# Attention before a two-layer MLP on one core: fewer transfers, float32 scores in the first batch, chained minima, keys copied by transfer, a cast on ScalarE

## The chip, the cores and the metric

One Trainium2 core. The metric is the device time of one execution in microseconds; the median of three runs of the kernel before is 1139.2 us (1138.72 to 1140.58).

## What is computed

Four batches, eight heads, 576 tokens, 64 columns a head; then two dense layers over the 2304 tokens with 512 columns.

```python
scores = scale * np.matmul(q, k.transpose(0, 1, 3, 2))
scores = np.where(causal, -1000000000.0, scores)
a = np.exp(scores - scores.max(-1, keepdims=True)); a /= a.sum(-1, keepdims=True) + 1e-09
local = np.matmul(a, v)
q_p = phi(q)                       # where(q > 0, q, exp(q) - 1) + 1
mem_ret = np.einsum('bhsd,bhde->bhse', q_p, M_prev)
mem_norm = np.einsum('bhsd,bhd->bhs', q_p, z_prev)[..., None] + 1e-06
attn = g * mem_ret / mem_norm + (1 - g) * local          # g = sigmoid(beta), per head
h = x @ w_in; y = np.where(h > 0, h, np.exp(np.minimum(h, 0)) - 1) @ w_out
h = y @ w2_in; out = np.maximum(0.01 * h, h) @ w2_out
```

The weights arrive as 64-bit floats and are decoded on the chip into a high and a low float32r part.

## The kernel before

**Precision by splitting.** Most products are made of float32r matmuls over a high part (a cast) and a low part (the rest), which one matmul more adds. Batch 0 (`full_v`, `ti < V32`) uses plain float32 for the weights times values, but not for the scores.

**Attention.** The work goes by pairs of heads, 16 in all. `load_qk` and `load_rest` issue a pair's loads through `load_rows` (L188): four transfers for each head of each of k, q and v, then z and M. All transfers of the kernel are issued on SP, one queue, in one order. `k_unit` (L255) transposes the keys on PE in two groups (256 and 320 rows), ScalarE casts them into both halves of `kk` (L266 and L267), VectorE makes the low part `kl` (L268). `q_unit` and `stacked` (L290) do the same for the queries, high part in one half of the 128 partitions, low part in the other (L299, L300). One score matmul over 128 partitions then gives (high + low) x high, a second one (L384) adds high x low of the keys. `score` masks and scales on VectorE with a running minimum of the negated scores (L386; the last block has two spans, whose minima L391 joins), and takes the exponential on ScalarE (L392). `norm` (L401 to L407) multiplies by the inverse sum on VectorE and GpSimd, `tr` transposes on PE, `pv` (L456) multiplies with values and memory and stores to DRAM scratch, for batches 1 to 3 in two stores of half the partitions each (L489, L490). `phi_unit` (L335) makes the memory's queries, with the gate's factor in L349 to L352.

**MLP.** The first layer's hidden columns are in 16 blocks of 128. Blocks 0 to 6 (`phase1_units`) are computed while the attention of later batches runs, once a batch is done: `u_x` loads the batch's half back from scratch, `u_h` makes a block's hidden values (`elu`, then `g_split`: high part by a cast, L582, which appears as L209, and low part on GpSimd, L583), `u_o` multiplies with the output weights after all seven. The rest of layer one and layer two follow after the attention. Decoding of the seven blocks' weights (`load_w`, L91) is spread over batch 0.

**What sets the order.** `weave` and `merge` write the units in an order of their costs, with credits for the MLP's units; a scheduler in the framework then places every engine's instructions by a simulated timeline, within priorities. So any edit can shift the order of all engines. Where a buffer is reused, it waits for its last reader: k, q and v have one buffer each.

Of the kernel before, what the change touches and what calls it, by code (L numbers as in the profile page):

```python
# [19 lines left out]
def _f(ap):  # L20
    return ap.bitcast(F32)
# [3 lines left out]
def kernel(  # L25
# [53 lines left out]
    gat = const.tile([P, H], F32, name="gat")  # L79
    omg = const.tile([P, H], F32, name="omg")  # L80
    nc.sync.dma_start(bet, beta.partition_broadcast(P))
    nc.scalar.activation(out=gat, in_=bet, func=AF.Exp, scale=-1.0)
    nc.vector.tensor_scalar(out=gat, in0=gat, scalar1=1.0, scalar2=None, op0=ALU.add)
    nc.vector.reciprocal(gat, gat)
# [52 lines left out]
    xo_scr = [dram.tile([P, NKC, tile_tok(t)[1]], F32, name=f"xo{i}") for i, t in enumerate(tiles1)]  # L137
# [31 lines left out]
    for par in range(2):  # L169
# [10 lines left out]
        nc.gpsimd.memset(d["m32"], 0.0)  # L180
        pads.append(d)
# [6 lines left out]
    def load_rows(dst, src, b, hp, ca, cb, dup):  # L188
        hs = slice(2 * hp, 2 * hp + 2)
        for j in range(2):  # L190
            h = 2 * hp + j
            cs = slice(j * D, (j + 1) * D)
            if ca == 0:
                nc.sync.dma_start(dst[:, 0:2, cs], src[b, h, 0:256, :].rearrange("(c p) d -> p c d", p=P))
            if cb == 5:
                nc.sync.dma_start(dst[0:64, 2, cs], src[b, h, 256:320, :])
                if dup:
                    nc.sync.dma_start(dst[64:128, 2, cs], src[b, h, 256:320, :])
                nc.sync.dma_start(dst[:, 3:5, cs], src[b, h, 320:576, :].rearrange("(c p) d -> p c d", p=P))
# [18 lines left out]
    class Pair:  # L218
# [12 lines left out]
        def load_qk(self):  # L231
            self.q = at.tile([P, 5, P], F32, tag="qn", bufs=1, name="qn")
            self.k = at.tile([P, 5, P], F32, tag="kn", bufs=1, name="kn")
            load_rows(self.k, k, self.b, self.hp, 0, self.cb, True)
            load_rows(self.q, q, self.b, self.hp, self.ca, self.cb, True)

        def load_rest(self):
            b, hp = self.b, self.hp
            self.v = at.tile([P, 5, P], F32, tag="vn", bufs=1, name="vn")
            load_rows(self.v, v, b, hp, 0, self.cb, True)  # L240
            self.z = at.tile([P, P], F32, tag="zb", bufs=1, name="zb")
            nc.sync.dma_start(
                self.z, z_prev[b, 2 * hp:2 * hp + 2, :].rearrange("h d -> (h d)").partition_broadcast(P)
            )
            self.mr = at.tile([P, 2, D], F32, tag="mr", bufs=1, name="mr")
            for r in range(2):
                nc.sync.dma_start(
                    self.mr[64 * r:64 * r + 64], M_prev[b, 2 * hp:2 * hp + 2].rearrange("h d e -> d h e")
                )
# [5 lines left out]
        def k_unit(self, grp):  # L255
            _, s0, n, cc = grp
            if s0 == 0:
                for j in range(2):
# [13 lines left out]
        def q_unit(self, grp):  # L272
            _, s0, n, cc = grp
            if grp is self.groups[0]:
# [60 lines left out]
        def phi_unit(self):  # L335
# [13 lines left out]
            nc.vector.tensor_scalar(out=den, in0=den, scalar1=1e-6, scalar2=None, op0=ALU.add)  # L349
            nc.vector.reciprocal(den, den)  # L350
            gb = gat[:, 2 * hp:2 * hp + 2].unsqueeze(1).to_broadcast([P, ncs, 2])
            nc.vector.tensor_tensor(out=den, in0=den, in1=gb, op=ALU.mult)  # L352
# [7 lines left out]
    class Item:  # L360
# [8 lines left out]
        def score(self, c):  # L369
# [3 lines left out]
            qs, kk, kl = pr.qs[j], pr.kk[j], pr.pad["kl", j]  # L373
# [18 lines left out]
            nc.scalar.activation(  # L392
                out=pt[0:m, 0:nk], in_=pt[0:m, 0:nk], func=AF.Exp, scale=-1.0, bias=mx[0:m, 0:1],
# [62 lines left out]
        def pv(self):  # L456
# [5 lines left out]
            pz = slice(64 - 64 * j, 128 - 64 * j)  # L462
# [26 lines left out]
            nc.sync.dma_start(xm_scr[pr.ti][ps, pr.hp, o:o + n], xp[ps])  # L489
            nc.sync.dma_start(xo_scr[pr.ti][ps, pr.hp, o:o + n], xp[pz])  # L490
# [117 lines left out]

    tail = False
# [7 lines left out]
    def phase1_units(ti):  # L617

        units = []
        for pi, (pt, o, w, _) in enumerate(parts):  # L620
# [4 lines left out]
            def u_x(pi=pi, o=o, w=w, st=st):  # L625
                xt = mtile("x", 1, F32, (NKC, NW))[:, :, 0:w]
                nc.sync.dma_start(xt, xm_scr[ti][:, :, o:o + w])
                if ti < V32:
                    st["x"] = split_x(xt, w, pi % 2)
# [3 lines left out]
                for c in range(NKC):  # L633
                    nc.sync.dma_start(x2[:, c], xo_scr[ti][:, c, o:o + w])
# [89 lines left out]
    attn.__exit__(None, None, None)  # L724
    wpb = ctx.enter_context(tc.tile_pool(name="wpb", bufs=1, side="right"))
# [149 lines left out]
```

## Time and profile before

| | us |
|---|---|
| median of 3 runs | 1139.2 |
| the profiled execution's own time | 1138.44 |
| its span, first to last instruction | 1136.4 |
| PE busy in it (share) | 1066.5 (94%) |
| DVE, ACT, POOL busy | 632.9, 517.0, 598.7 |
| mean granted clock of TensorE | 0.977 |

The span is a few us shorter than the execution's time; differences of times are taken against the latter. PE is TensorE's matmuls, PEld its weight loads, DVE VectorE, ACT ScalarE, POOL GpSimd, SPq the queue of SP from which transfers are issued. A busy PE is modelled from pipelined matmuls: starts tell more than ends. A float32 matmul leaves two records. In the chain of waits a row is what held the end at that time: an instruction, an issue, or a transfer in flight.

### The profile page before, as it was taken

The page shows a single profiled execution, that of the slowest core. Times are in us where ns is not written, and L with a number is a line of the kernel's source. Part 1 is how long each engine was busy: PE and PEld are TensorE (multiplying, and loading weights), DVE is VectorE, ACT ScalarE, POOL GpSimd, SP SyncE. Part 2 cuts the span into 40 slices and gives each one's busy share as a digit, 9 for nine tenths or more (in the row PEclk, how much of TensorE's full clock was granted, in tenths as well). Part 3 has the DMA queues.
Part 4 walks back from the last instruction along what each step waited for, and adds up shares of the span by engine and source line. Part 5 has one row for each costly group of instructions (what it writes and reads, how often), then busy time and mean ns, then how long its engine had stood idle before and what let it go on. Part 6 is the DMA issues. An engine that isn't in the chain of part 4 may idle for free.

```text
span 1136.4 us, 17760 instructions
## 1 busy us (share of the span) xinstructions
PE 1066.5 (94%) x5904; PEld 925.5 (81%) x5904; DVE 632.9 (56%) x1470; ACT 517.0 (45%) x1236; POOL 598.7 (53%) x720
## 2 busy tenths in 40 slices
PE   4887889998999999898999999999999999999998
PEld 2765779997989899886877788988888888888887
DVE  6678798779897974765656431566331232231232
ACT  5897877776787763545444232433211111111110
POOL 5778676666666752677668333575532332322222
PEclk8998889999999999998999999999999999999999
DMA  3455233444344524654364430343010020010010
GB/s 97 98 158 145 66 89 78 108 118 109 85 108 116 148 53 139 207 169 141 131 197 132 128 93 20 110 151 111 19 56 1 14 62 1 1 38 1 1 38 19
DMA packets 146906, 100.92 MB, mean 89 GB/s; under 512 B 84480, under 2 KB 140800, under 8 KB 146816
## 3 DMA queue, kind: packets, MB, share of 16 engines
q1 hardware_dynamic: 146816, 99.80, 30.7%
q8 instruction: 47, 0.77, 0.3%
q14 instruction: 43, 0.35, 0.1%
HBM read 73.80 MB, written 25.95 MB: 88 GB/s over the span
## 4 chain that ended last, share of the span: by engine, by line
PE 59%; DVE 12%; DMA 9%; POOL 7%; ACT 5%; issue 5%; SPq 3%; DVEq 0%; ACTq 0%; POOLq 0%
PE sc L823 13%; PE pm L576 13%; PE tp L576 11%; PE sc L604 5%; PE po L823 4%; PE pm L604 3%; PE po L481 3%; PE tp L413 2%; POOL w L120 2%; POOL xv L758 2%; DVE pt L386 2%; DMA wraw<-in_moe_w_out_dram 2%; PE po L604 2%; POOL gl L583 1%; DVE wm L111 1%
## 5 line engine op out<-in xcount | busy, mean ns | idle before, releaser
L583 POOL TENSOR_TENSOR gl<-e,gh 128x512 fp32r<-128x512 f32 (+2 forms) x181 | 205.1, 1136 | 334.1 <-DVE gh L209 286.8
L576 PE MATMUL tp<-xw,w 128*128 128x512 f32 (+1 forms) x504 | 146.0, 371 | 3.8 <-DVE e L590 3.8
L576 PE MATMUL pm<-xw,w 128*128 128x512 f32 (+1 forms) x496 | 142.2, 368 | 0.0
L823 PE MATMUL sc<-w,gh 128*128 128x512 f32 x448 | 136.2, 390 | 0.0
L407 POOL TENSOR_SCALAR pt<-pt,rs,omg 128x128 f32<-128x128 f32 (+4 forms) x160 | 109.4, 693 | 18.5 <-DVE rs L402 15.6
L604 PE MATMUL sc<-gh,w 128*128 128x512 f32 (+2 forms) x438 | 105.9, 343 | 6.1 <-DVE gh L209 2.5
L576 PEld LDWEIGHTS tp<-xw,w 128*128 128x128 f32 x504 | 92.7, 191 | 20.5 <-DVE e L590 4.2
L392 ACT ACTIVATE pt<-pt,mx 128x128 f32<-128x128 f32 (+4 forms) x160 | 93.0, 582 | 32.8 <-DVE mx L386 24.1
L120 POOL TENSOR_TENSOR w<-wm,w 128x512 fp32r<-128x512 f32 x64 | 84.2, 1336 | 44.6 <-ACT w L207 37.6
L576 PEld LDWEIGHTS pm<-xw,w 128*128 128x128 f32 x496 | 90.7, 188 | 16.4
L209 DVE CAST gh<-e 128x512 fp32r<-128x512 f32 (+2 forms) x181 | 92.3, 513 | 19.4 <-PE po L604 6.1
L823 PEld LDWEIGHTS sc<-w,gh 128*128 128x128 f32 x448 | 83.1, 188 | 16.5
L413 PE MATMUL tp<-ident,pt 128*128 128x128 f32 x480 | 84.6, 286 | 11.6 <-POOL pt L407 3.8
L576 PE MATMUL tp<-xv,w 128*128 128x512 f32 (+1 forms) x252 | 93.5, 371 | 0.0
L576 PE MATMUL pm<-xv,w 128*128 128x512 f32 (+1 forms) x248 | 91.4, 369 | 0.0
L386 DVE CUSTOM_DVE_ANT_0 pt<-sc,mask 128x128 f32<-128x128 f32 (+2 forms) x192 | 82.6, 446 | 15.4 <-PE sc L384 10.0
L595 ACT ACTIVATE e<-pm 128x512 f32<-128x512 f32 (+1 forms) x40 | 22.2, 556 | 147.6 <-PE pm L576 147.6
L604 PEld LDWEIGHTS sc<-gh,w 128*128 128x128 f32 x438 | 74.8, 189 | 17.1 <-DVE gh L209 3.5
L823 PE MATMUL sc<-w,gl 128*128 128x512 f32 x224 | 84.6, 389 | 0.0
L576 PE MATMUL pm<-xh,w 128*128 128x288 f32 x368 | 79.1, 305 | 5.0 <-ACT xh L207 3.2
L596 DVE TENSOR_TENSOR e<-tp,e 128x512 f32<-128x512 f32 (+1 forms) x40 | 25.5, 636 | 104.1 <-ACT e L595 104.1
L383 PE MATMUL sc<-kk,qs 128*128 128x256 f32 (+2 forms) x192 | 71.4, 377 | 12.7 <-DVE mx L386 7.4
(142 smaller groups left out, 2469.2 us busy)
## 6 DMA issues: line engine op xcount, KB each, us to landing
wraw<-in_moe_w_in_dram SPq DMA_DIRECT2D x32, 512.0 KB, 4.1
wraw<-in_moe_w_out_dram SPq DMA_DIRECT2D x32, 512.0 KB, 5.0
x<-xm SPq DMA_DIRECT2D x8, 576.0 KB, 4.6
ys<-st SPq DMA_DIRECT2D x32, 144.0 KB, 2.7
x1s<-st SPq DMA_DIRECT2D x36, 128.0 KB, 1.9
x<-x1s SPq DMA_DIRECT2D x9, 512.0 KB, 3.7
out_dram<-st SPq DMA_DIRECT2D x36, 128.0 KB, 1.7
kn<-in_k_dram SPq DMA_DIRECT2D x64, 64.0 KB, 2.2
```

Source lines behind the costliest of these rows:

```text
L120: nc.gpsimd.tensor_tensor(out=w[:, 1, a], in0=t[:, a], in1=_f(w)[:, 0, a], op=ALU.subtract)
L209: (nc.vector if eng == "V" else nc.gpsimd).tensor_copy(dst, src)
L383: nc.tensor.matmul(o, qs[:, c0:c0 + P], kk[:, k0:k0 + npad], start=True, stop=False)
L386: nc.vector.tensor_tensor_reduce(out=pt[0:m, k0:k0 + n], in0=sc[0:m, 0:n], in1=mk, op0=ALU.add, op1=ALU.min, scale=-0.125, scalar=1e38, ac ...
L392: nc.scalar.activation(out=pt[0:m, 0:nk], in_=pt[0:m, 0:nk], func=AF.Exp, scale=-1.0, bias=mx[0:m, 0:1], accum_out=self.pd["ss"][0:m, c:c ...
L407: nc.gpsimd.tensor_scalar(out=pt, in0=pt, scalar1=rs[0:m, i:i + 1], scalar2=omg[0:m, h:h + 1], op0=ALU.mult, op1=ALU.mult,)
L413: nc.tensor.transpose(dst, self.p[c][:, k0:k0 + kn], ident)
L481: nc.tensor.matmul(po[:, a:b], w, x, start=i == 0, stop=i == len(mms) - 1)
L576: nc.tensor.matmul(ph, wi[:, wj, kc, :], xx[:, kc, :], start=n_mm == 0, stop=n_mm == 11)
L583: nc.gpsimd.tensor_tensor(out=gl, in0=g, in1=_f(gh), op=ALU.subtract)
L604: nc.tensor.matmul(py, wo[:, wj, ec * P:(ec + 1) * P], gg, start=opens and f == first and n_mm == 0, stop=closes and f == last and n_mm == 2,)
L823: nc.tensor.matmul(pos[tb], gg[:, tb * P:(tb + 1) * P], wo[:, wj, :], start=f == 0 and n_mm == 0, stop=f == NF - 1 and n_mm == 2,)
```

## The change

1. `load_rows` issues two transfers per head for keys and queries (their middle 64 rows come within a block of 128, without a second copy of them), and six per pair for values; z and M are loaded for two pairs at once.
2. In batch 0 the keys are copied as float32, both heads in one tile, the queries into tiles whose other half is zero, and a span's score is one float32 matmul of just its columns. The zeros are set once on GpSimd.
3. In batches 1 to 3 the keys' second copy in the other half of `kk` is a transfer on SP in place of a ScalarE cast.
4. The second span's minimum starts from the first span's, in place of the instruction that joined them; the gate enters with the same instruction that adds 1e-6, as its inverse (`ging`).
5. `pv` of batches 1 to 3 stores all partitions in one transfer; `u_x` reads the right halves back in four transfers in place of five.
6. The MLP's cast to `gh` is on ScalarE while the attention is being written, 35 of the 56 blocks there, and stays on VectorE after it.

```diff
-    def load_rows(dst, src, b, hp, ca, cb, dup):
+    def load_rows(dst, src, b, hp, dup):
         hs = slice(2 * hp, 2 * hp + 2)
...
+        for ca, cb, r0 in ((0, 2 if dup else 3, 0), (3, 5, 320)):
+            for j in range(2):
+                nc.sync.dma_start(
+                    dst[:, ca:cb, j * D:(j + 1) * D],
+                    src[b, 2 * hp + j, r0:r0 + (cb - ca) * P, :].rearrange("(c p) d -> p c d", p=P),
+                )
+        for r in range(2 if dup else 0):
+            nc.sync.dma_start(
+                dst[64 * r:64 * r + 64, 2, :].rearrange("p (j d) -> p j d", j=2),
+                src[b, hs, 256:320, :].rearrange("j p d -> p j d"),
+            )
...
         def k_unit(self, grp):
...
+            if self.full_v:
+                nc.scalar.copy(_f(self.kk[0])[:, s0:s0 + n], tp[:, 0:n])
+                return
             for j, ps, po in self.heads():
                 kk = self.kk[j]
                 nc.scalar.copy(kk[ps, s0:s0 + n], tp[ps, 0:n])
-                nc.scalar.copy(kk[po, s0:s0 + n], tp[ps, 0:n])
+                nc.sync.dma_start(_f(kk)[po, s0:s0 + n], _f(kk)[ps, s0:s0 + n])
...
         def q_unit(self, grp):
             _, s0, n, cc = grp
+            if self.full_v:
...
+                for j, ps, po in self.heads():
+                    self.qs[j] = self.pad["q32", j]
+                    copy("V" if j else "A", self.qs[j][ps, s0:s0 + n], tp[ps, 0:n])
+                return
...
-            nc.vector.tensor_scalar(out=den, in0=den, scalar1=1e-6, scalar2=None, op0=ALU.add)
+            gb = ging[:, 2 * hp:2 * hp + 2].unsqueeze(1).to_broadcast([P, ncs, 2])
+            nc.vector.scalar_tensor_tensor(out=den, in0=den, scalar=1e-6, in1=gb, op0=ALU.add, op1=ALU.mult)
             nc.vector.reciprocal(den, den)
...
-            nc.vector.tensor_tensor(out=den, in0=den, in1=gb, op=ALU.mult)
...
-                nc.tensor.matmul(o, qs[:, c0:c0 + P], kk[:, k0:k0 + npad], start=True, stop=False)
-                nc.tensor.matmul(o, qs[:, c0:c0 + P], kl[:, k0:k0 + npad], start=False, stop=True)
+                if pr.full_v:
+                    nc.tensor.matmul(sc[:, 0:n], qs[:, c0:c0 + P], _f(kk)[:, k0:k0 + n], start=True, stop=True)
+                else:
+                    nc.tensor.matmul(o, qs[:, c0:c0 + P], kk[:, k0:k0 + npad], start=True, stop=False)
+                    nc.tensor.matmul(o, qs[:, c0:c0 + P], kl[:, k0:k0 + npad], start=False, stop=True)
...
-                    scale=-0.125, scalar=1e38, accum_out=mx[0:m, i:i + 1],
+                    scale=-0.125, scalar=mx[0:m, 0:1] if i else 1e38, accum_out=mx[0:m, i:i + 1],
...
-            if c == 4:
-                nc.vector.tensor_tensor(out=mx[:, 0:1], in0=mx[:, 0:1], in1=mx[:, 1:2], op=ALU.min)
...
-            nc.sync.dma_start(xm_scr[pr.ti][ps, pr.hp, o:o + n], xp[ps])
-            nc.sync.dma_start(xo_scr[pr.ti][ps, pr.hp, o:o + n], xp[pz])
+            nc.sync.dma_start(xq_scr[pr.ti][j][:, pr.hp, o:o + n], xp)
...
-        copy(E_GH, gh, g)
+        copy("A" if attending else E_GH, gh, g)
...
-                for c in range(NKC):
-                    nc.sync.dma_start(x2[:, c], xo_scr[ti][:, c, o:o + w])
+                for j in range(2):
+                    ps, pz = slice(64 * j, 64 * j + 64), slice(64 - 64 * j, 128 - 64 * j)
+                    nc.sync.dma_start(xt[ps], xq_scr[ti][j][ps, :, o:o + w])
+                    nc.sync.dma_start(x2[ps], xq_scr[ti][j][pz, :, o:o + w])
```

The queue of SP at its start, before (kn, qn, vn are a pair's keys, queries and values, wraw the raw weights):

```order
L194 DMA kn<-in_k_dram 128x2x64
L196 DMA kn<-in_k_dram 64x64
L198 DMA kn<-in_k_dram 64x64
L199 DMA kn<-in_k_dram 128x2x64
...
L196 DMA qn<-in_q_dram 64x64
L198 DMA qn<-in_q_dram 64x64
L199 DMA qn<-in_q_dram 128x2x64
L194 DMA vn<-in_v_dram 128x2x64
L101 DMA wraw<-in_moe_w_in_dram 128x4x256
```

and with the change:

```order
L199 DMA kn<-in_k_dram 128x3x64 x2
L199 DMA kn<-in_k_dram 128x2x64 x2
L199 DMA qn<-in_q_dram 128x3x64 x2
L199 DMA qn<-in_q_dram 128x2x64 x2
L199 DMA vn<-in_v_dram 128x2x64
L102 DMA wraw<-in_moe_w_in_dram 128x4x256
```

Ahead of the first value and weight transfers stand 8 loads in place of 16.

The same queue where the second pair of batch 1 is prepared, with the change (kk is the keys' tile, xm the scratch of batch 0):

```order
L286 DMA kk_1483<-kk_1483 64x256
L286 DMA kk_1484<-kk_1484 64x256
L199 DMA kn<-in_k_dram 128x3x64 x2
L199 DMA kn<-in_k_dram 128x2x64
L286 DMA kk_1483<-kk_1483 64x320
L514 DMA xm_80<-xp 64x320
L286 DMA kk_1484<-kk_1484 64x320
L199 DMA kn<-in_k_dram 128x2x64
```

The four copies stand between the next pair's key loads and a store of an earlier item.

ScalarE's queue at the first pair, before:

```order
L266 CAST kk_211<-sc 64x256
L267 CAST kk_211<-sc 64x256
L266 CAST kk_212<-sc 64x256
L267 CAST kk_212<-sc 64x256
L266 CAST kk_211<-sc 64x320
L267 CAST kk_211<-sc 64x320
L266 CAST kk_212<-sc 64x320
L267 CAST kk_212<-sc 64x320
L299 CAST qs_232<-sc 64x256
L299 CAST qs_233<-sc 64x256
```

and with the change:

```order
L281 COPY kk_214<-sc 128x256
L281 COPY kk_214<-sc 128x320
L226 COPY q_0_161<-sc 64x256
L370 ACTIVATE ph_e<-qn 128x640
L226 COPY q_0_161<-sc 64x320
```

Eight casts of keys became two copies, and each query group has one copy here, the other on VectorE.

## Rows read from the trace of the kernel before

**Rows 1.** Busy time by stretch: us, busy us (instructions), clock, DMA share, GB/s.

```profile
0.00:161.00 161.00, 123.64 (x612) 96.64 (x613) 120.76 (x336) 125.67 (x324) 113.55 (x173) 0.88 0.43 111
161.00:440.00 279.00, 265.02 (x1980) 254.07 (x1979) 232.43 (x700) 203.80 (x573) 180.35 (x278) 0.99 0.39 99
640.00:1136.00 496.00, 490.79 (x2356) 414.06 (x2354) 157.38 (x283) 96.70 (x179) 173.77 (x160) 1.00 0.13 42
```

**Rows 2.** Chain of waits, 0 to 161 us: start us, us, what.

```profile
1.16 0.42 SPq L194
...
10.41 0.47 SPq L194
10.92 4.51 DMA wraw<-in_moe_w_in_dram
...
28.47 0.25 SPq L194
...
60.04 7.73 DMA wraw<-in_moe_w_out_dram
...
81.31 5.04 DMA wraw<-in_moe_w_out_dram
...
125.52 0.62 SPq L198
```

**Rows 3.** Chain of waits, 161 to 440 us, shares by line.

```profile
by line: PE pm L604 14.0%; PE po L481 8.7%; PE pm L576 7.8%; PE tp L413 6.6%; issue 4.9%; DVE pt L386 4.0%; DMA x<-xm 3.4%; PE sc L383 3.0%; PE sc L384 2.8%; ACT pt L392 2.5%; DVE qs L300 2.0%; DVE al L216 2.0%; PE tp L576 1.8%; DVE dl L216
```

**Rows 4.** Timeline from 9 us: start, us, engine, line, what, [idle before <- releaser].

```profile
10.68 1.09 PE L296 MATMUL sc<-ident,qn 128*128 128x128 f32 x3 [2.53 <-DMA qn<-in_q_dram]
```

**Rows 5.** Groups by line: count, busy us, mean ns, idle before it.

```profile
L173 POOL MEMSET kl<- 64x576 f32 x4 | 2.3, 573 | 0.2
...
L267 ACT CAST kk<-sc 64x256 fp32r<-64x256 f32 (+1 forms) x64 | 25.2, 394 | 0.8
...
L268 DVE TENSOR_TENSOR kl<-sc,kk 64x256 fp32r<-64x256 f32 (+1 forms) x64 | 28.8, 451 | 12.4 <-ACT kk L267 11.6
...
L488 DVE COPY xp<-po 128x256 f32<-128x256 f32 (+1 forms) x48 | 21.5, 448 | 5.1 <-PE po L481 4.7
...
L391 DVE TENSOR_TENSOR mx<-mx 128x1 f32<-128x1 f32 x32 | 13.7, 429 | 0.1
```

**Rows 6.** Waits, 0 to 161 us: total us, times, longest us.

```profile
POOL rs L401 <- ACT pt L392: 21.2, 12, 7.8
...
ACT wm L109 <- DMA wraw<-in_moe_w_out_dram: 4.2, 3, 1.9
```

**Rows 7.** Timeline of PE from 41.5 us.

```profile
41.88 1.03 PE L481 MATMUL pm<-d,vv 128*128 128x256 f32 x4
42.74 0.49 PE L413 MATMUL tp<-ident,pt 128*128 128x128 f32 x3
...
43.31 0.28 PE L383 MATMUL sc<-kk,qs 128*128 128x256 f32 x1
43.43 0.28 PE L384 MATMUL sc<-kl,qs 128*128 128x256 f32 x1
```

**Rows 8.** Groups of DVE by line and shape, 161 to 440 us.

```profile
L209 DVE CAST gh<-e 128x288 fp32r<-128x288 f32 x41 | 17.7, 434 | 0.4
```

**Rows 9.** Transfers of the whole run: count, KB each, median us to landing.

```profile
xm<-xp SPq DMA_DIRECT2D x32, 64.0 KB, 2.0
```

**Rows 10.** Timeline, first and twelfth pair of batches 1 to 3.

```profile
112.49 0.42 ACT L267 CAST kk<-sc 64x320 fp32r<-64x320 f32 x1
...
114.14 0.47 PE L383 MATMUL sc<-kk,qs 128*128 128x256 f32 x1
...
395.41 0.42 ACT L267 CAST kk<-sc 64x320 fp32r<-64x320 f32 x1
...
400.72 0.28 PE L383 MATMUL sc<-kk,qs 128*128 128x256 f32 x1
```

**Rows 11.** Waits of SP's queue, 161 to 440 us: total us, times, longest.

```profile
SPq L489 <- DVE mx L386: 9.8, 10, 3.9
```

More of the change, by code (lines that the diff above doesn't have):

```diff
@@ L79 @@
     gat = const.tile([P, H], F32, name="gat")
+    ging = const.tile([P, H], F32, name="ging")
     omg = const.tile([P, H], F32, name="omg")
     nc.sync.dma_start(bet, beta.partition_broadcast(P))
-    nc.scalar.activation(out=gat, in_=bet, func=AF.Exp, scale=-1.0)
-    nc.vector.tensor_scalar(out=gat, in0=gat, scalar1=1.0, scalar2=None, op0=ALU.add)
-    nc.vector.reciprocal(gat, gat)
+    nc.scalar.activation(out=ging, in_=bet, func=AF.Exp, scale=-1.0)
+    nc.vector.tensor_scalar(out=ging, in0=ging, scalar1=1.0, scalar2=None, op0=ALU.add)
+    nc.vector.reciprocal(gat, ging)
     nc.vector.tensor_scalar(out=omg, in0=gat, scalar1=-1.0, scalar2=1.0, op0=ALU.mult, op1=ALU.add)
@@ L136 @@
     xm_scr = [dram.tile([P, NKC, tile_tok(t)[1]], F32, name=f"xm{i}") for i, t in enumerate(tiles1)]
-    xo_scr = [dram.tile([P, NKC, tile_tok(t)[1]], F32, name=f"xo{i}") for i, t in enumerate(tiles1)]
+    xq_scr = [
+        [dram.tile([P, NKC, tile_tok(t)[1]], F32, name=f"xq{i}_{j}") for j in range(2)] for i, t in enumerate(tiles1)
+    ]
     x_scr = [
@@ L180 @@
         nc.gpsimd.memset(d["m32"], 0.0)
+        for j in range(2):
+            d["q32", j] = pools["wst"].tile([P, S], F32, tag=f"q32{j}_{par}", name=f"q32{j}_{par}")
+            nc.gpsimd.memset(d["q32", j][64 - 64 * j:128 - 64 * j], 0.0)
         pads.append(d)
@@ L239, in load_rest @@
             self.v = at.tile([P, 5, P], F32, tag="vn", bufs=1, name="vn")
[L240 to L249, printed above, removed]
+            load_rows(self.v, v, b, hp, True)
+            if hp % 2 == 0:
+                load_memory(b, 2 * hp)
+            zb, mr = memory_in[b, hp]
+            h0 = 2 * (hp % 2)
+            self.z = zb[:, h0 * D:h0 * D + P]
+            self.mr = mr[:, h0:h0 + 2, :]
         def heads(self):
@@ L257, in k_unit @@
             if s0 == 0:
-                for j in range(2):
+                for j in range(1 if self.full_v else 2):
                     self.kk[j] = at.tile([P, S], F32R, tag=f"kk{j}", bufs=2, name=f"kk{j}")
@@ L273, in q_unit @@
             _, s0, n, cc = grp
+            if self.full_v:
+                tp = bank("sc")
+                for c in cc:
+                    c0, m = CH[c]
+                    nc.tensor.transpose(tp[:, c0 - s0:c0 - s0 + P], self.q[:, c, :], ident)
+                for j, ps, po in self.heads():
+                    self.qs[j] = self.pad["q32", j]
+                    copy("V" if j else "A", self.qs[j][ps, s0:s0 + n], tp[ps, 0:n])
+                return
             if grp is self.groups[0]:
@@ L387, in score @@
                     out=pt[0:m, k0:k0 + n], in0=sc[0:m, 0:n], in1=mk, op0=ALU.add, op1=ALU.min,
-                    scale=-0.125, scalar=1e38, accum_out=mx[0:m, i:i + 1],
+                    scale=-0.125, scalar=mx[0:m, 0:1] if i else 1e38, accum_out=mx[0:m, i:i + 1],
                 )
-            if c == 4:
-                nc.vector.tensor_tensor(out=mx[:, 0:1], in0=mx[:, 0:1], in1=mx[:, 1:2], op=ALU.min)
+            last = len(spans) - 1
             nc.scalar.activation(
-                out=pt[0:m, 0:nk], in_=pt[0:m, 0:nk], func=AF.Exp, scale=-1.0, bias=mx[0:m, 0:1],
+                out=pt[0:m, 0:nk], in_=pt[0:m, 0:nk], func=AF.Exp, scale=-1.0, bias=mx[0:m, last:last + 1],
                 accum_out=self.pd["ss"][0:m, c:c + 1],
@@ L607, in o_mm @@
                 )
+    attending = True
     tail = False
@@ L724 @@
     attn.__exit__(None, None, None)
+    attending = False
     wpb = ctx.enter_context(tc.tile_pool(name="wpb", bufs=1, side="right"))
```

29 lines of the change are left out of this document (13 added, 16 removed).

## The prediction

> **What bounds the kernel now.** I began with busy times by stretch [rows 1]. From 640 to 1136 us PE is busy 490.8 of 496 us: there the kernel is its matmuls, and no edit touches them. Between 440 and 640 us lies the rest of the MLP's first layer with its weight decode; the change touches none of that either. So what can move lies in the first 440 us, and whatever is gained there moves the rest forward unchanged, as the work of both later stretches is the same.
>
> Stretch A (0 to 161 us, until the first matmul of the MLP) has no full engine: DVE 120.8, ACT 125.7, POOL 113.6 and PE 123.6 of 161 us, at a granted clock of 0.88. An engine's share does not say here what a saving is worth; the chain of waits does [rows 2]. I summed its pieces from 0 to 161 us by engine: 31.7 us DVE (54 pieces), 24.1 us SPq (46), 33.9 us transfers in flight (9), 22.1 us PE (35), 21.0 us ACT (37), 8.6 us POOL (5). The reader is to see that SP, which computes nothing, holds the end for 24 us by issuing alone. It issues one transfer after another, 0.42 to 0.59 us each, and the weights that the decode waits for stand in the same queue: the row at 60.04 is 7.73 us in which the chain is only a weight transfer, the row at 81.31 another 5.04 us, the one at 10.92 another 4.51 us.
>
> Stretch B (161 to 440 us, batches 1 to 3 woven with the MLP) has PE busy 265.0 of 279 us, so at most some 14 us of plain idleness are to be had, more where a matmul waits behind another's operand. Its chain (the 200 longest of 780 pieces, its lines in [rows 3]) still has 40.7 us DVE, 14.9 us ACT, 19.7 us transfers and 7.0 us SPq beside 90.1 us PE.
>
> **The change, part by part, stretch A.**
>
> *Fewer transfers.* A pair's keys, queries and values take 8 issues each now and 4, 4 and 6 then; z and M take 3 each pair now and 3 each second pair then. At the start 18 pieces of SPq up to 10.9 us stand in the chain, 9.4 us or 0.52 us each, the first and the last of them in [rows 2]; the first q transpose waits 2.53 us for its transfer and starts at 10.68 [rows 4]. The order shows 8 issues instead of 16 ahead of the first value and weight transfer: 8 x 0.52 = **-4.2 us**. The four added clears on POOL cost 573 ns each like the present kl clears [rows 5], 2.3 us, beside POOL's longest wait for an exponential, 7.8 us, which is its first [rows 6]: nothing, and 2.3 us if that cover goes. After the start 21 more pieces of loads (L194 to L199) lie in the chain, 11.1 us, first and last in [rows 2]; 24 loads become 14, so 10/24 of it: **-4.6 us**. The bounds are nothing (another row of the queue takes each place) and the whole 11.1 us. The rows say that an issue holds SP for about half a microsecond, and I take that. The Trainium skill ("DMA: Bandwidth & Descriptors", Anatomy of one DMA — SWDGE (gpsimd) path) gives about 50 ns for the sequencer's dispatch, for transfers issued by GpSimd; by that the two terms would shrink from 8.8 to about 0.8 us and the forecast would be 1124. The rows of SP contradict 50 ns tenfold, and the measurement decides.
>
> The weight transfers in the chain (17.3 us in three pieces) come earlier when fewer loads stand ahead. How much of their landing then disappears behind other work no row shows: nothing at one end, 12.8 us (the two later pieces) at the other. I take **-3 us**, near the low end, since ACT waited only 4.2 us in all for them [rows 6].
>
> *Float32 scores in batch 0.* Per pair, ACT loses 8 key casts and 2 of 4 query casts, 394 ns each, and gets 2 full-width copies of the same columns, priced alike: -3.2 us. DVE loses 4 kl and 4 qs subtractions, 451 ns each, and gets 2 query copies, 448 ns as the xp copy: -2.7 us [rows 5]. *Chained minima* take away one instruction of 429 ns per head: -0.9 us a pair. *The gate's factor* takes away one small instruction on ten columns, priced like a minimum: -0.4 us. Over four pairs that is 12.6 us ACT and 16.0 us DVE. With some 2.5 pairs of batch 1 prepared in A (ACT loses 4 second key casts, DVE the minima and the gate) it is 16.5 of ACT's 125.7 us (13%) and 19 of DVE's 120.8 us (16%). Taken from their pieces of the chain in the same shares: 2.7 + 5.1 = **-7.8 us**. The bounds are 0, if other waits step in, and 35.5 us, if all of it was on the path.
>
> PE pays. Two float32 matmuls of 256 columns take 0.86 us from start to start (four records, 41.88 to 42.74), so 0.43 us each; a float32r one takes 0.12 us (43.31 to 43.43) [rows 7]. A head's six spans are 1856 columns twice now, 2 x 1856/256 x 0.12 = 1.74 us, and 1728 columns in float32 then, 1728/256 x 0.43 = 2.90 us. Eight heads: +9.3 us of PE. PE is 22.1 of A's 161 us in the chain, 14%, so I count **+1.3 us**; the bounds are 0 and 9.3 us at this clock.
>
> A: -4.2 - 4.6 - 3 - 7.8 + 1.3 = **-18.3 us**.
>
> **Stretch B.** 35 of the 56 gh casts go from DVE to ACT: 35 x 434 ns [rows 8] = 15.2 us off DVE. Minima and gate over 9.5 pairs: 9.5 x 1.29 = 12.2 us. Together 27.4 of DVE's 232.4 us, 12%, of 40.7 us in the chain: **-4.9 us**. On ACT the casts add 15.2 us and the 4 second key casts of 9.5 pairs take away 15.0 us: 0; behind it a cast can now queue behind exponentials, covered because a block's g is used only after all seven. On SP a pair has 35 transfers now (27 loads, 8 stores) and 23.5 then (15.5 loads, 4 copies of keys, 4 stores): a third less of 7.0 us, **-2.3 us**. Against it stands the keys' second copy, 394 ns on ACT today, by transfer then. No row shows a transfer inside the chip's memory; the nearest is 2.0 us for an xp store of the same 64 KB [rows 9], plus an issue of 0.5 us. Today the second-half copy is ready 3.6 us before the pair's first score in the mean of 12 pairs, 1.2 us in the first of them (112.91 to 114.14) and 4.9 us in the last (395.83 to 400.72) [rows 10], and scores over the first 256 keys need only the first half, so most of it is hidden: I take **+2 us**, between 0 and the +29 us of the rival below. B: **-5 us**.
>
> Sum: -23 us against the profiled execution's 1138.4 us (span 1136.4). That run stands 0.8 us under the median, 1139.2, and against the median it is **1116 us**.
>
> **The rivals.** *POOL paces A.* POOL loses nothing, and it is 113.6 of 161 us busy. If its normalisation is what every item waits for, the ACT and DVE savings turn into waits on it, and only the two SP terms remain: 1139.2 - 8.8 = 1130. For it: 71% busy, and next in size. Against it: it idles 21.2 us waiting for the exponentials [rows 6] and is 8.6 us of A's chain.
>
> *The keys' copy comes late (slower).* SP serves its queue in order. A copy stands behind whatever SP is waiting for: in B it stood 10 times before an xp store (L489), up to 3.9 us at once [rows 11]. A copy held 3.9 us, issued (0.5) and landed (2.0) takes 6.4 us against 0.4 us today, so it is 6.0 us later; the mean lead covers 3.6 us of that, and PE would stand 2.4 us in each of 12 pairs, with the MLP's matmuls queued behind: +29 us. With the other terms (-25) that is 1143. It decides from a mean hold of about 3.6 us, where the loss in a pair reaches 25/12 = 2.1 us. For it: nothing in the queue goes around a wait. Against it: fewer loads stand in the queue, and 3.9 us is the longest hold there, not the mean (9.8 us in 10 times).
>
> *The savings were hidden anyway.* The order of every engine moves, the pieces of the chain are replaced by their neighbours, and the time stays within the noise: 1139.
>
> **How the numbers follow.** First case 0.62 (1116), POOL 0.18 (1130), late copies 0.13 (1143), hidden 0.07 (1139). Low end: the SP, weight and ACT/DVE terms at twice their value, 1096. High end: up to the hidden case, 1140; the late copies stay out. About 0.2%, 2.3 us, is what a measurement of this kernel can tell from no change. Faster 0.80, same 0.07, slower 0.13.
>
> **What would show it.** Right: the first matmul of the MLP starts at about 143 us, SPq falls under 15 us in the chain of A, ACT and DVE lose 13 and 16% there, PE in the float32 scores takes about 2.9 us a head, the stretch after the attention keeps its length. Wrong: scores waiting for a kk transfer for over 1 us a pair, POOL over 85% busy in A, or a first MLP matmul still at 160 us.

## The result and the profile after

The changed kernel takes 1123.2 us (median of 4 runs, 1122.8 to 1124.8) beside 1139.9 us for the kernel before: a ratio of 0.9859, with a 95% interval of 0.9844 to 0.9874. That is 1.4% faster. Of its stages, by the profiled executions:

| us | before | after | difference |
|---|---|---|---|
| first matmul of the MLP (end of stretch A) | 161.1 | 132.8 | -28.3 |
| last store of the attention issued | 442.8 | 419.1 | -23.7 |
| from there to the end | 693.6 | 702.3 | +8.7 |
| span | 1136.4 | 1121.4 | -15.0 |

So the attention gave 23.7 us, and 8.7 us were lost again in a stretch whose instructions the change does not touch. Busy time by stretch after [rows 1] (us, then busy us and instructions of PE, PEld, DVE, ACT and POOL, then clock, DMA share, GB/s):

```profile
0.00:133.00 133.00, 108.87 (x551) 81.45 (x552) 94.03 (x261) 96.35 (x248) 110.14 (x163) 0.97 0.52 137
133.00:420.00 287.00, 274.76 (x2063) 266.86 (x2063) 228.72 (x669) 209.72 (x605) 187.31 (x293) 0.98 0.42 108
...
620.00:1121.00 501.00, 495.68 (x2345) 411.13 (x2343) 154.65 (x282) 95.30 (x177) 172.75 (x159) 1.00 0.13 42
```

Three things are to be seen. POOL, 113.6 of 161 us before, is now 110.1 of 133 us (83%) and the fullest engine of stretch A. PE's granted clock there is 0.97 in place of 0.88, so more of the stretch runs at 2.4 GHz and less at 1.2. And the boundary between the stretches has moved within the work: 550 records of matmuls lie before the first MLP matmul now, 612 before, as the third pair of batch 1 is only partly prepared by then. Over both stretches PE has 2614 records in either kernel. Up to 443 us it was busy 391.7 us and idle 51.3 (the window of [rows 1] ends 3 us earlier); now, up to 420 us, 383.6 and 36.4. So 15 of these 23 us are idle time gone, and 8 are PE's busy time, although the float32 scores take longer. The clock alone does not explain the 8: run e2 below, in the order of the kernel before, has 0.94 in its first 160 us, and its attention ends only 2.4 us sooner (440.4). What does was not found.

The chain of waits of stretch A after (start us, us, what) [rows 2]:

```profile
5.31 0.47 SPq L199
...
5.82 0.47 SPq L102
...
6.88 5.37 DMA wraw<-in_moe_w_out_dram
...
46.93 6.12 POOL pt L436 x5
...
64.10 4.22 POOL w L121 x2
...
126.89 5.42 DMA x<-xm
```

Summed over all its pieces by engine, before and after: SPq 24.3 and 14.0 us, transfers 33.9 and 16.6, DVE 33.7 and 6.2, ACT 21.7 and 18.8, PE 26.8 and 35.3, POOL 8.6 and 32.0. Beside PE the chain now runs through the normalisation (L436) and the weights' low parts (L121) on POOL, where it ran through VectorE, loads and weight transfers. POOL's wait for exponentials, 21.2 us before [rows 6], has nearly gone; ScalarE's for weights has shrunk a little (waits, 0 to 133 us: total us, times, longest):

```profile
POOL rs L430 <- ACT pt L421: 3.7, 2, 2.6
...
ACT wm L110 <- DMA wraw<-in_moe_w_out_dram: 2.9, 3, 1.6
```

The start went as forecast. PE's timeline from 3 us (start, us, engine, line, what, [idle before <- releaser]) [rows 4]:

```profile
4.15 1.51 PE L279 MATMUL sc<-ident,kn 128*128 128x128 f32 x5 [4.15 <-DMA kn<-in_k_dram]
6.38 1.57 PE L297 MATMUL sc<-ident,qn 128*128 128x128 f32 x5 [0.73 <-DMA qn<-in_q_dram]
7.75 2.56 PE L411 MATMUL sc<-kk,q 128*128 128x128 f32 x6
```

The first q transpose starts at 6.38 us in place of 10.68, the first score at 7.75. The keys' copies by transfer land when they were expected to (count, KB each, median us to landing) [rows 9], and never late. The tightest pair is the second of batch 1 (timeline of all engines): its last copy, of the keys behind the first 256, is issued at 118.84 and lands at 120.93, and its first score, which needs only the first 256 keys, starts at 120.34. No score waits for such a copy anywhere in the waits of the kernel.

```profile
kk<-kk SPq DMA_DIRECT2D x24, 80.0 KB, 2.1
kk<-kk SPq DMA_DIRECT2D x24, 64.0 KB, 2.0
```

```profile
118.84 0.55 SPq L286 DMA_DIRECT2D kk<-kk  x1
...
120.34 0.37 PE L413 MATMUL sc<-kk,qs 128*128 128x256 f32 x1
```

Where are the 8.7 us? In the later stretch, the same matmuls are slower one by one, at a granted clock of 1.00 in both. Groups of PE by line and shape from 520 to 680 us, of before (count, busy us, mean ns of one):

```profile
L576 PE MATMUL pm<-xw,w 128*128 128x512 f32 x112 | 35.1, 389 | 0.0
```

and of the changed kernel:

```profile
L603 PE MATMUL pm<-xw,w 128*128 128x512 f32 x113 | 35.9, 395 | 0.0
```

From start to start the difference is the same: 0.227 us before, 0.233 us now, in the mean over the 512-column matmuls of the rest of layer one. In layer two it goes by block. The median distance from start to start, in ns, of the matmuls with x of blocks 0 to 15, second group of tokens, worked out from the starts in the traces:

```
before 227 227 227 227 227 227 227 227 227 227 227 227 227 227 227 227
after  230 227 227 227 227 227 227 234 234 234 234 234 234 234 234 234
```

Blocks 7 to 15 are slow, and all of layer one's rest has those blocks too. The kernel takes its tiles from two ends of the on-chip memory, `side="left"` and `side="right"`. The weights of these blocks lie on the right; x, gh and the first seven blocks' weights lie on the left. The one part of the change that moves them is the 32-byte tile `ging`: it pushed all that lies on the left 32 bytes further.

### The profile page after: what moved, and what is told of

Its sections match the earlier page's. It is cut to its first block, busy times and chain, and to the rows that moved or that the text cites. A ratio compares the mean times of both kernels' runs of the same rounds, so it can differ in the third digit from the quotient of the medians.

```text
span 1121.4 us, 17423 instructions
## 1 busy us (share of the span) xinstructions
PE 1066.8 (95%) x5904; PEld 917.1 (82%) x5904; DVE 600.0 (54%) x1363; ACT 493.9 (44%) x1191; POOL 599.9 (53%) x724
## 4 chain that ended last, share of the span: by engine, by line
PE 69%; DMA 9%; POOL 7%; DVE 6%; ACT 4%; issue 4%; SPq 2%; DVEq 0%; POOLq 0%; ACTq 0%
PE pm L603 16%; PE sc L854 14%; PE tp L603 12%; PE sc L631 5%; PE po L854 4%; PE pm L631 4%; PE po L509 3%; PE tp L442 3%; POOL w L121 2%; DMA x<-xq 2%; PE po L631 2%; PE pm L509 2%; DMA wraw<-in_moe_w_out_dram 1%; PE sc L413 1%; PE sc L414 1%
## 5 line engine op out<-in xcount | busy, mean ns | idle before, releaser
L610 POOL TENSOR_TENSOR gl<-e,gh 128x512 fp32r<-128x512 f32 (+2 forms) x181 | 202.0, 1119 | 348.7 <-DVE gh L228 304.3
L603 PE MATMUL tp<-xw,w 128*128 128x512 f32 (+1 forms) x504 | 147.0, 374 | 5.5 <-DVE e L617 5.5
L603 PE MATMUL pm<-xw,w 128*128 128x512 f32 (+1 forms) x496 | 143.8, 371 | 0.0
L854 PE MATMUL sc<-w,gh 128*128 128x512 f32 x448 | 137.7, 393 | 0.0
L436 POOL TENSOR_SCALAR pt<-pt,rs,omg 128x128 f32<-128x128 f32 (+4 forms) x160 | 107.2, 679 | 19.4 <-DVE rs L431 15.8
L603 PEld LDWEIGHTS tp<-xw,w 128*128 128x128 f32 x504 | 92.2, 190 | 24.3 <-DVE e L617 6.0
L121 POOL TENSOR_TENSOR w<-wm,w 128x512 fp32r<-128x512 f32 x64 | 87.5, 1387 | 37.3 <-ACT w L226 37.1
L603 PEld LDWEIGHTS pm<-xw,w 128*128 128x128 f32 x496 | 90.5, 188 | 18.4
L421 ACT ACTIVATE pt<-pt,mx 128x128 f32<-128x128 f32 (+4 forms) x160 | 93.4, 585 | 23.4 <-DVE mx L416 21.7
L603 PE MATMUL tp<-xv,w 128*128 128x512 f32 (+1 forms) x252 | 93.9, 373 | 0.0
L603 PE MATMUL pm<-xv,w 128*128 128x512 f32 (+1 forms) x248 | 92.0, 371 | 0.0
L228 DVE CAST gh<-e 128x512 fp32r<-128x512 f32 (+2 forms) x146 | 76.5, 527 | 20.4 <-PE po L631 7.5
L442 PE MATMUL tp<-ident,pt 128*128 128x128 f32 x480 | 79.3, 277 | 8.3 <-ACT ah L232 3.2
L623 DVE TENSOR_TENSOR e<-pm,e 128x512 f32<-128x512 f32 (+1 forms) x40 | 25.5, 636 | 106.7 <-ACT e L622 106.6
L603 PE MATMUL pm<-xh,w 128*128 128x288 f32 x368 | 80.1, 303 | 2.1 <-ACT xh L226 1.7
L416 DVE CUSTOM_DVE_ANT_0 pt<-sc,mask 128x128 f32<-128x128 f32 (+4 forms) x160 | 69.0, 448 | 12.1 <-PE tp L442 6.0
```

The source lines that it names most:

```text
L121: nc.gpsimd.tensor_tensor(out=w[:, 1, a], in0=t[:, a], in1=_f(w)[:, 0, a], op=ALU.subtract)
L228: (nc.vector if eng == "V" else nc.gpsimd).tensor_copy(dst, src)
L416: nc.vector.tensor_tensor_reduce(out=pt[0:m, k0:k0 + n], in0=sc[0:m, 0:n], in1=mk, op0=ALU.add, op1=ALU.min, scale=-0.125, scalar=mx[0:m, ...
L421: nc.scalar.activation(out=pt[0:m, 0:nk], in_=pt[0:m, 0:nk], func=AF.Exp, scale=-1.0, bias=mx[0:m, last:last + 1], accum_out=self.pd["ss"] ...
L436: nc.gpsimd.tensor_scalar(out=pt, in0=pt, scalar1=rs[0:m, i:i + 1], scalar2=omg[0:m, h:h + 1], op0=ALU.mult, op1=ALU.mult,)
L442: nc.tensor.transpose(dst, self.p[c][:, k0:k0 + kn], ident)
```

## The experiments

Ratios are to the kernel before, timed beside each run, and the changed kernel stands at 0.9859. Stage times are those of each run's profile.

**Is it the position? (e1, e2, e3, e5, e6.)** An unused tile moves the left side in the changed kernel (e1) and in the kernel before (e2):

```diff
-    omg = const.tile([P, H], F32, name="omg")
+    omg = const.tile([P, H], F32, name="omg"); pad = const.tile([P, H], F32, name="pad"); nc.gpsimd.memset(pad, 0.0)
```

e3 has the same tile on the right side, ahead of the attention's tiles; e6 has 96 bytes on the left (`[P, 3 * H]`); e5 needs no new tile:

```diff
-    ging = const.tile([P, H], F32, name="ging")
+    ging = bet
```

Apart from one clear on GpSimd, the order of every engine's instructions is that of the kernel it is made from (e5 has no such clear).

> The changed kernel with one more unused tile of 32 bytes per partition among the constants, on the side where the first seven blocks' weights, x and gh lie; every engine's order is the same but for one clear on GpSimd. The change's own new 32-byte tile (ging) had moved all that lies on that side from 32 to 0 mod 64 bytes, while the weights of blocks 7 to 15 on the other side stayed at 32 mod 64; in the trace of the changed kernel the matmuls that pair the two sides start about 5 to 7 ns further apart than before. Theory position (operands of one matmul at unlike places in 64 bytes go slower): both sides are at 32 mod 64 again, 512-column matmuls start 0.227 us apart everywhere, and the time falls by 8 to 13 us, to 1110 to 1115. Rival (the wider spacing comes from something else, as the activity before it or the new order of the work): 1123 within 2 us, spacing as in the changed kernel.

> The kernel before with an unused tile of 32 bytes per partition among the constants; nothing else differs but one clear on GpSimd. Theory position: the left side moves to 0 mod 64, the matmuls that pair it with blocks 7 to 15 start 0.23 to 0.235 us apart in place of 0.227, and the time rises by 8 to 13 us, to 1147 to 1153. Rival (the spacing comes from the new order): no change, 1139.5 within 2 us.

> The changed kernel with the unused 32-byte tile on the other side, ahead of the attention's tiles, the weights of blocks 7 to 15 and x: now both sides are at 0 mod 64. Theory position as a difference between the two operands: fast, 1110 to 1115, spacing 0.227 everywhere, as with the tile on the left. Rival within it, position by itself (a tile at 0 mod 64 is slow, whatever the other): no better than the changed kernel, 1123 or up to 10 us slower. Rival order: 1123 within 2 us.

> The changed kernel with the gate's inverse kept in the tile of beta, so that no new tile is there and every later tile of the left side lies where it lay in the kernel before (96 mod 128 bytes, as the weights of blocks 7 to 15 on the other side). So far the stretch from the last attention store to the end took 694 us with the two sides at the same place in 128 bytes (the kernel before), 702 and 702 us at 32 bytes apart, 698 and 699 us at 64 bytes apart. Theory position: 694 us again, 512-column matmuls 0.227 us apart everywhere, 1114 to 1118. Rival (a new order of the work is what slows that stretch in the changed kernel): 1121 to 1124.

> The changed kernel with an unused tile of 96 bytes among the constants: the left side lies 128 bytes further than in the kernel before, at the same place in 128 bytes as the other side, and not in 256. Theory period of 128 bytes: as e5, 1114 to 1118, spacing 0.227 everywhere. Rival (only the very addresses of before are fast, a longer period): 1119 to 1124, spacing wider in some of the blocks.

| run | left side against right side, bytes from before | ns of one (L603 pm<-xw) | from the last store to the end, us | time, us | ratio (95%) |
|---|---|---|---|---|---|
| before | 0 | 389 | 693.6 | 1139.9 | 1 |
| after | +32 | 395 | 702.3 | 1123.2 | 0.9859 (0.9844 to 0.9874) |
| e1 | +64 | 391 | 698.3 | 1122.4 | 0.9863 (0.9844 to 0.9882) |
| e2, from before | +32 | 395 | 701.3 | 1144.6 | 1.0062 (1.0044 to 1.0079) |
| e3 | +64 | 391 | 699.4 | 1120.6 | 0.9847 (0.9827 to 0.9866) |
| e5 | 0 | 389 | 694.0 | 1118.1 | 0.9819 (0.9800 to 0.9838) |
| e6 | +128 | 394 | 702.8 | 1124.7 | 0.9874 (0.9854 to 0.9895) |

The rows behind the third column, for e2 and for e5:

```profile
L576 PE MATMUL pm<-xw,w 128*128 128x512 f32 x112 | 35.8, 395 | 0.0
```

```profile
L603 PE MATMUL pm<-xw,w 128*128 128x512 f32 x120 | 37.4, 389 | 0.0
```

e2 settles that it is position: an unused tile of 32 bytes costs the kernel before 0.6% (7 us), with its order unchanged, and its later stretch grows from 693.6 to 701.3 us. e5 settles that it explains the loss: with the left side back in place the stretch is 694.0 us, the time falls to 1118.1 us, and the interval lies wholly below that of the changed kernel. By the ratios the whole kernel gains some 4.6 us of the 8.3 that the stretch gives back in the profiled execution; in e1, e3, e5 and e6 the last store comes 1 to 3 us later than in the changed kernel's profile, with the same order. **By its median e5 is the fastest version.** e1 and e3 have different positions, but the same difference between the two sides (a tile on the right, which is filled from its other end, counts like one on the left), the same 391 ns, and block for block the same steps in layer two: what counts is how the sides lie to each other. My rule was too simple, though. I had expected e1 to be as fast as e5 (same place in 64 bytes); it recovered half of what the stretch had lost (in layer two its blocks 7 to 15 lie between 229 and 233 ns), and nothing that its total could tell. Then I expected e6 to be fast (same place in 128 bytes); it is as slow as the changed kernel. What period the positions have, and what in the chip waits, stays open.

**The keys' copy (e4, e9) and the gh cast (e8, e7).** e4 takes the copies back to ScalarE:

```diff
                 nc.scalar.copy(kk[ps, s0:s0 + n], tp[ps, 0:n])
-                nc.sync.dma_start(_f(kk)[po, s0:s0 + n], _f(kk)[ps, s0:s0 + n])
+                nc.scalar.copy(kk[po, s0:s0 + n], tp[ps, 0:n])
```

> The changed kernel with the keys' second copy in batches 1 to 3 made by ScalarE again in place of the transfer (48 copies of about 392 ns, 18.8 us on ScalarE; 48 issues fewer on SP). Theory hidden: the trace shows no score that waits for such a transfer, so the transfer costs nothing and gives ScalarE some room: undoing it costs 0 to 5 us, 1123 to 1128. Rival late copies: the copies stand behind stores on SP and hold scores back, so undoing it gains over 3 us, under 1120.

e4: 1137.6 us (1134.0 to 1142.7), ratio 0.9993 (0.9978 to 1.0007). That is 1.3%, 15 us, slower than the changed kernel: nearly its whole gain is gone. Stretch A is nearly as before the edit (134.4 us), the loss lies in batches 1 to 3, whose last store comes at 437.2 in place of 419.1 us. Neither theory had it: the direction is that of the hidden case, the size three times its upper end. Late copies are out. e8 puts the gh cast on VectorE again, e7 both:

```diff
-        copy("A" if attending else E_GH, gh, g)
+        copy(E_GH, gh, g)
```

> The changed kernel with the gh cast on VectorE throughout; the keys' copies stay a transfer. The prediction's terms: 35 casts of 434 ns go back to VectorE, 15.2 us, of which its share of the chain gives about 3 us: 1126. Theory ScalarE's load: ScalarE gets still freer by 15 us, so no loss or a gain, 1116 to 1124. Rival VectorE's load: 1128 or more.

> The changed kernel with the keys' second copy on ScalarE and the gh cast on VectorE throughout, both as before. The run with the copies alone on ScalarE again was 1.3% slower than the changed kernel. Theory ScalarE's load (with both jobs ScalarE is too late for matmuls that wait on it): the gh casts are taken off it again, so most of that loss goes, 1122 to 1128. Rival (the loss is in the copies themselves, as they hold the score bank and kk, whatever else ScalarE does): 1133 or more.

e8: 1129.2 us, ratio 0.9916 (0.9898 to 0.9934), 6.5 us slower than the changed kernel, as the rival of VectorE's load had it. Only 1.7 us of it stand at the attention's last store and some 1.3 are ten more matmuls left over for later (0.13 us each). Most of the rest are waits of PE where layer one ends, in code that the edit does not touch: from 520 to 640 us it is idle for 2.9 us in the changed kernel and for 7.2 in e8 (PE's busy time by stretch, first of the changed kernel, then of e8):

```profile
520.00:560.00 40.00, 39.74 (x171) 1.00 0.50 158
560.00:640.00 80.00, 77.36 (x329) 1.00 0.39 125
```

```profile
520.00:560.00 40.00, 37.79 (x161) 1.00 0.46 137
560.00:640.00 80.00, 75.06 (x318) 1.00 0.40 129
```

e7: 1134.8 us, ratio 0.9959 (0.9945 to 0.9974), so taking the casts off ScalarE again does not bring back what the copies cost; the rival's 1133 holds. The four kernels form a table. With the keys' copies by transfer, the gh cast on ScalarE gains 6.5 us (0.9916 to 0.9859); with the copies on ScalarE it loses 4 us (0.9959 to 0.9993). So the cast is worth something on ScalarE only once the copies are off it. Busy time from 134.4 to 438 us in e4:

```profile
134.40:438.00 303.60, 281.90 (x2078) 272.75 (x2079) 238.04 (x677) 227.23 (x648) 187.90 (x296) 0.97 0.36 93
```

and from 133 to 431 us in e7:

```profile
133.00:431.00 298.00, 278.67 (x2063) 270.11 (x2064) 245.02 (x716) 219.13 (x614) 189.87 (x296) 0.97 0.37 95
```

ScalarE is 227.2 of 303.6 us busy in e4, 75%, and 219.1 of 298 in e7, 74%; in the changed kernel it is 73%. No engine is full, and still the copies' 18.8 us on ScalarE cost 15 us with the casts on it (e4 beside the changed kernel) and 5 without them (e7 beside e8). Together the two parts are worth 11 us (e7 beside the changed kernel). e9 asks whether it is ScalarE's load or the place of the copies, which stood ahead of the second head's cast and so kept the bank of the transposed keys:

```diff
                 nc.scalar.copy(kk[ps, s0:s0 + n], tp[ps, 0:n])
-                nc.sync.dma_start(_f(kk)[po, s0:s0 + n], _f(kk)[ps, s0:s0 + n])
...
+            for j, ps, po in self.heads():
+                kk = self.kk[j]
+                nc.scalar.copy(kk[po, s0:s0 + n], _f(kk)[ps, s0:s0 + n])
```

> The changed kernel with the keys' second copy on ScalarE again, but read from kk and behind both first casts, so that the bank of the transposed keys comes free as soon as with the transfer; ScalarE's load is that of e4 (1.3% slower than the changed kernel). Theory bank (the copies held a score bank and the low parts behind them): most of the loss goes, 1123 to 1128. Rival ScalarE (the copies stand in its queue ahead of what PE and the others wait for, wherever they read from): 1132 or more.

e9: 1130.3 us (1125.6 to 1133.5), ratio 0.9916 (0.9891 to 0.9941), between the two. With the same copies on ScalarE as in e4, the later place, and reading from `kk`, win back over half of the loss (the bank's theory), and 6.5 us stay (ScalarE's). The scheduler also moves the instructions of all engines with each of the edits e4 and e7 to e12, and no run tells a part's own worth from that of the new order. So I take this split, and the size of each single part, as rough; e8 shows some 4 us of waits in a stretch whose code is the same.

**The loads (e11).** `load_rows`, `load_qk` and `load_rest` as before, eight transfers a pair for each of k, q and v, and z and M for each pair.

```diff
...
-            load_rows(self.k, k, self.b, self.hp, False)
-            load_rows(self.q, q, self.b, self.hp, False)
+            load_rows(self.k, k, self.b, self.hp, 0, self.cb, True)
+            load_rows(self.q, q, self.b, self.hp, self.ca, self.cb, True)
...
```

> The changed kernel with the loads of k, q, v, z and M as before (27 a pair in place of 15.5 on average). The prediction's terms: 4.2 us at the start, 4.6 later in the first stretch, 3 for weights that land later, some 2 in the stretch of batches 1 to 3: 1137. Rival (after the start another row of the queue or another engine holds the chain): 1124 to 1129.

e11: 1159.0 us (1158.5 to 1159.9), ratio 1.0172 (1.0151 to 1.0192). That is 36 us slower than the changed kernel, 2.6 times my terms, and even slower than the kernel before. Stretch A ends at 166.2 us, where it ended at 161.1 before. Its busy times:

```profile
0.00:166.00 166.00, 129.36 (x623) 97.16 (x624) 108.41 (x297) 108.85 (x282) 124.89 (x181) 0.90 0.43 113
```

VectorE and ScalarE have 12 and 17 us less to do in A than before [rows 1], and A is not a microsecond shorter. That the loads alone bring A back to its old length points at the queue of SP as what held it. Counted over its issues up to 130 us, SP spends 104 us issuing in the kernel before (192 transfers), 108 in e11 (195) and 79 in the changed kernel (153). A piece of e11's chain of waits shows it, four issues to a head (two heads here), each some half a microsecond, one behind the other:

```profile
25.53 0.47 SPq L200
...
26.05 0.48 SPq L202
...
26.57 0.59 SPq L204
...
27.20 0.59 SPq L205
...
27.89 0.41 SPq L200
...
28.35 0.48 SPq L202
...
28.87 0.60 SPq L204
...
29.51 0.59 SPq L205
```

The transfers of the changed kernel are no slower to issue, though they carry more (instructions of line 199 up to 130 us: count, ns min/median/max, first and last start):

```profile
L199 SPq DMA_DIRECT2D kn<-in_k_dram x28: 368/480/1872, 1.2 to 119.4; - x28
L199 SPq DMA_DIRECT2D qn<-in_q_dram x28: 369/474/520, 3.2 to 125.0; - x28
```

Its 28 issues for keys are seven pairs' loads, at four a pair; in e11 a pair takes eight. And it goes on behind the attention: e11 has 476 matmuls of the first seven blocks left then, the changed kernel 393; at 0.13 us each that is 11 us. This is also why e11 is slower than the kernel before: the last store comes at 442.1 us, as there (442.8), but 87 more matmuls are left behind it (11 us), and the wider spacing of the blocks 7 to 15 is still in it. The same loads issued from a second queue, which would tell SP's issuing from the landing of the transfers, were not tried.

**The scores and the minima (e10, e12).** e10 makes the scores of batch 0 from float32r parts again, with the keys' second copy on ScalarE there; e12 has the separate minimum and the separate product with the gate again (of each edit the main lines):

```diff
...
-                if pr.full_v:
-                    nc.tensor.matmul(sc[:, 0:n], qs[:, c0:c0 + P], _f(kk)[:, k0:k0 + n], start=True, stop=True)
-                else:
-                    nc.tensor.matmul(o, qs[:, c0:c0 + P], kk[:, k0:k0 + npad], start=True, stop=False)
-                    nc.tensor.matmul(o, qs[:, c0:c0 + P], kl[:, k0:k0 + npad], start=False, stop=True)
+                nc.tensor.matmul(o, qs[:, c0:c0 + P], kk[:, k0:k0 + npad], start=True, stop=False)
+                nc.tensor.matmul(o, qs[:, c0:c0 + P], kl[:, k0:k0 + npad], start=False, stop=True)
```

```diff
-            gb = ging[:, 2 * hp:2 * hp + 2].unsqueeze(1).to_broadcast([P, ncs, 2])
-            nc.vector.scalar_tensor_tensor(out=den, in0=den, scalar=1e-6, in1=gb, op0=ALU.add, op1=ALU.mult)
+            nc.vector.tensor_scalar(out=den, in0=den, scalar1=1e-6, scalar2=None, op0=ALU.add)
...
+            nc.vector.tensor_tensor(out=den, in0=den, in1=gb, op=ALU.mult)
...
-                    scale=-0.125, scalar=mx[0:m, 0:1] if i else 1e38, accum_out=mx[0:m, i:i + 1],
+                    scale=-0.125, scalar=1e38, accum_out=mx[0:m, i:i + 1],
...
+            if c == 4:
+                nc.vector.tensor_tensor(out=mx[:, 0:1], in0=mx[:, 0:1], in1=mx[:, 1:2], op=ALU.min)
...
```

> The changed kernel with the scores of batch 0 by float32r parts again (casts, low parts and two matmuls a span as before, the second copy on ScalarE there). The prediction's terms: ScalarE gets 12.6 us and VectorE 10.8 us more in the first stretch, of which their shares of the chain are 2.1 and 2.9 us; PE loses 9.3 us, 1.3 us of the chain: 1127. Rival PE (the float32 scores hold the first stretch): faster than the changed kernel, under 1120. Rival full weight (ScalarE and VectorE each hold the stretch): 1133 or more.

> The changed kernel with the separate minimum of the last block's two spans and the separate product with the gate, as before: 48 small VectorE instructions of some 0.43 us more, 20.6 us. The prediction's terms: 2.3 us in the first stretch and 2.2 in that of batches 1 to 3: 1128. Rival hidden: 1121 to 1125.

e10: 1133.7 us (1128.2 to 1134.9), ratio 0.9940 (0.9916 to 0.9963), 9 us slower than the changed kernel. The first MLP matmul comes at 141.1 us, 8.3 later. So the float32 scores gain although PE pays for them, which rules out that they hold A. The size, over twice my term of 3.7 us, is at the bound that I had set for the full weight of ScalarE and VectorE; but as in e8 some of it are waits of PE where layer one ends (idle for 6.2 us from 520 to 640 us, in place of 2.9), and the second copies on ScalarE are in it too. e12: 1134.3 us (1130.6 to 1140.2), ratio 0.9953 (0.9934 to 0.9972), 10.7 us slower; A ends at 137.7 us, and the attention's last store comes 8.3 us later. Hidden is out: 20.6 us of small instructions, on an engine that is 71 and 80% busy in the changed kernel's two stretches, cost half their length.

## Why the prediction was right, and where it was not

The forecast was 1116 us (1096 to 1140) with 0.80 for faster; the result, 1123.2, lies in the range and on the side foreseen.

- **The sum held to the end of the attention and failed behind it.** I forecast -23 us there, and it is -23.7. The step that failed is "whatever is gained there moves the rest forward unchanged". e2 and e5 show why: the change added a tile, the tile moved the operands of some 2000 later matmuls against each other, and that stretch lost 8.7 us. Without that displacement (e5) the kernel takes 1118.1 us, 2 us from the forecast. That the sum up to there is met so closely is luck in good part: its two halves missed by 10 us each, in opposite directions, and some of the single parts by more, as the next points show.
- **The split into A and B was off.** A fell by 28.3 us (forecast 18.3), B grew by 4.6 (forecast -5), and the first MLP matmul came at 132.8 us, not 143. Some of A's fall is the boundary: most of a pair of batch 1 that was prepared in A is prepared in B now, 62 records of matmuls. Of the signs that I named, VectorE and ScalarE lost 22 and 23% of their time in A in place of 16 and 13, for that reason too. The price of the float32 scores held: a span of 288 columns takes 0.49 us from start to start, which is 2.9 us a head. The stretch after the attention did not keep its length.
- **Loads, -8.8 us in A, with 3 us for the weights and most of 2.3 us in B.** The start gave what was priced: 4.3 us at the first q transpose (10.68 to 6.38) for 4.2. SPq fell to 14.0 us in A's chain, under the 15 named. But as a whole the term was far too small: 14 us with its share of B, where e11 shows 36 when the loads alone are put back. I summed SP's 24 us in the chain and took a share of them; I did not count that SP issued for 104 of the first 130 us, and called the stretch one without a full engine. The Trainium skill ("DMA: Bandwidth & Descriptors", Anatomy of one DMA — SWDGE (gpsimd) path) has about 50 ns for the dispatch on GpSimd's path. By it the term would have shrunk; the issues on SP, which is another path, took 0.41 to 0.60 us in the rows above, and the term grew.
- **The keys' copy, +2 us.** The sign was wrong. Its landing time (2.0 us) was right, its lead was enough, and no score waits for it. But I set ScalarE's balance to 0, 15.2 us of casts against 15.0 us of copies, and put at nothing that the copies on ScalarE keep the bank of the transposed keys: e4 shows 15 us, of which e9 lays over half on that bank. The two belong together, as e7 and e8 show.
- **ACT and DVE, -7.8 us in A and -4.9 in B, and PE +1.3.** Taken back one at a time these parts cost 9 us (scores, 3.7 by my terms), 10.7 (minima and gate, 4.5) and 6.5 (gh, 2.7). The direction held, the sizes were two to three times too small. A share of the chain is what is visible on the path before; it supposes that the next engine in line does not gain with it, which was not tested. In B the share was also taken of the 200 longest pieces alone: they hold 40.7 us of VectorE, all 780 hold 71.4, and by these the term would be -8.4 in place of -4.9. The clock in A (0.88 before, 0.97 after) accounts for little of it: e2, in the order of before, has 0.94 there and ends A at 159.8 us in place of 161.1. A small size was off too: the second span's instruction with the chained minimum takes 507 ns against 448 ns for the first, so a head saves 0.37 us, not 0.43.
- **The parts do not add.** Taken back alone, the five cost 15 + 6.5 + 36 + 9 + 11 = 77 us, over three times what the change gave in the attention. My reading is that once all the others are in, each one that is put back becomes what the rest waits for; the new orders of the scheduler are in these numbers too. That each would give as little when it is put alone into the kernel before was not tried, and the fifth point of the change (stores in one transfer, four reads in place of five) was not taken back by itself.
- **The rivals.** POOL did become the fullest engine in A, 83%, and its chain grew from 8.6 to 32.0 us, but after the savings and not in their place. Late copies are ruled out by e4, hidden savings by the result.

## What to carry to other kernels

Count a queue that issues transfers as an engine: the sum of its issue times over a stretch tells how full it is (here 104 of 130 us), though no table of busy times lists it. Where several engines are nearly balanced, a part's share of the path before came out two to three times too small here; what it is worth there shows when it is taken back from the finished version. And after a change compare the mean time of one matmul in the stretches that it does not touch; a new constant can move every tile behind it, and a tile that is no longer needed may have room for it.

## What I had not expected of the hardware

Matmuls of 512 columns with one operand on each side of the memory start 0.227 us apart in the kernel before and 0.233 us apart after a displacement of 32 bytes, at the same granted clock (1.00); of 64 bytes, 391 ns for one in place of 389 and 395. The Trainium skill ("SBUF — State Buffer", SBUF: two separate sides) says that among the engines only the pair of ports that VectorE and GpSimd share can make one wait, and that PE never waits on anyone. The left and right of this kernel are the two ends of the memory, and not the sides of that section's title. No run here shows what PE is held up by. But e2 and e5 show that its pace depends on where its operands lie to each other, 7 us in 1140, which that sentence does not lead one to expect; whether it is wrong or only silent on this stays open.
